# A decode kernel's output row: two column groups instead of four, the residual added on TensorE, the copy split over two engines, and two one-row stores

## The chip, the cores and the metric

The kernel runs on one core of a Trainium2 chip. A core has a matrix engine (PE, with its weight loads shown apart as PEld), a vector engine (DVE), a scalar engine (ACT), a general engine (POOL), a sequencer that mostly issues transfers (SP), and 16 DMA engines that move data between the chip's memory (HBM) and the on-chip memory (SBUF). Matmul results land in a separate accumulation memory, PSUM, which DVE and ACT read. Engines run their own instruction streams and wait for each other on semaphores.

The metric is the device time of one execution in microseconds. Before the change it is 128.65 us (median of three runs, 128.65 to 128.98). The profile is of another single execution, which took 128.68 us.

## What is computed

One token is decoded through two branches that share a normalised input, and both are added to the residual:

```python
xn = _layernorm(x)                       # x is (1, 1, 576)
# branch A: attention over the last W = 4096 cached positions, 32 query heads, 16 key/value heads
q = (xn @ wq).reshape(B, Sq, 32, 128)
p = _softmax(einsum(q, k[:, :, Sk - W:]) * 128 ** -0.5)
A = (einsum(p, v[:, :, Sk - W:])).reshape(B, Sq, 4096) @ wo
# branch B: a gated MLP
z = _gelu(xn @ w_in)                     # 4608 wide
z1, z2 = z[..., :2304], _layernorm(z[..., 2304:])
B = (z1 * (w_sp * z2 + b_sp)) @ w_out
out = x + A + B                          # (1, 1, 576), bfloat16
```

Nearly all of the work is reading: 16 heads of keys and of values (1 MB each), wq, w_in, w_out and wo come to 51 MB for one row of output.

## The kernel before

**Loads.** All large loads are issued by SP, in program order, into a ring of seven equal SBUF slots (`RING`, line 60): wq in two pieces, the first two pairs of K heads, w_in in three pieces, then pairs of K and V heads in turn (lines 83 to 86, issued at L85), w_out in one piece and wo in four pieces of 16, 10, 4 and 2 tiles (`load_n`, lines 88 to 91 and 105, issued at L90). A tile of wo is 128 rows of 576 columns; each partition of a piece of n tiles reads n x 1152 contiguous bytes. A load that reuses a slot waits until the engine that read the slot's old contents is done: DVE for a pair of K heads, PE for a pair of V heads. A slot is handed out in the order in which slots come free in the program. SP's queue is in order, so a load that waits holds back those behind it. The small loads go out from ACT's queue: x as 64 rows of 9 (`x64`), x as four rows of 144 (`x4`, lines 111 to 114, after a memset by DVE), and two scalars (`spb`).

**Main loop** (line 380, over 16 K heads). `t_head` (L247) transposes a K head with DVE, `s_head` (L255) makes scores on the PE, `sm_a` and `sm_b` do the softmax of a group of four heads with DVE and ACT, `pv` (L305) multiplies with V, and `yb` brings the group's result into `Y`. In between lies branch B: `z_mms` at head 3, `z_rest` at head 5, `z_norm` at head 6. `z_norm` sums over partitions with a matmul into a PSUM tile of its own, `psz`, taken from the pool `ps_m`, and ends in `hv`, the 2304 gated values. At head 5 the output accumulator `out_t`, 144 columns wide, is taken from the pool `ps_a` and zeroed (L393).

**The output.** The output row of 576 columns is kept as four groups of `CW` = 144 columns. `out_mms` (L403) multiplies one tile of w_out or wo, with one column of `hv` or `Y` as weights, in four matmuls, one for each group; group n writes partition 32n of `out_t`, and its `tile_position` puts it on a separate group of 32 columns of the PE array. After the loop come the last group's softmax, `yb(2)`, `pv(3)`, two thirds of w_out, `yb(3)`, the last third of w_out and the 32 tiles of wo, piece by piece as they land. The end is one DVE instruction (L425), which adds `x4` to `out_t` over 97 partitions and writes bfloat16, and one store from SP (L426) of the four rows at partitions 0, 32, 64 and 96.

**Order.** The kernel's order is written by hand (`manual_schedule`): each engine runs its instructions as the Python code issues them. The waits between engines are put in by the tile framework. It also gives the transfers eight semaphores in turn; a transfer waits until the earlier one on its semaphore has landed.

Of the kernel before, what the change touches and what calls it, by code (L numbers as in the profile page):

```python
# [8 lines left out]
FP32 = mybir.dt.float32  # L9
BF16 = mybir.dt.bfloat16  # L10
ALU = mybir.AluOpType
# [3 lines left out]
D = 576  # L15
# [11 lines left out]
NG = HKV // GK  # L27
NR = 98
NF = FH // 128
CW = D // 4  # L30
EPS = 1e-5
SCALE = DH ** -0.5
GELU_C = 0.7978845608028654
# [6 lines left out]
def kernel(  # L40
# [14 lines left out]
    nc = tc.nc  # L55
    P = nc.NUM_PARTITIONS

    const = ctx.enter_context(tc.tile_pool(name="const", bufs=1))
# [5 lines left out]
    ps_m = ctx.enter_context(tc.tile_pool(name="ps_m", bufs=1, space=bass.MemoryType.PSUM))  # L64
    ps_a = ctx.enter_context(tc.tile_pool(name="ps_a", bufs=1, space=bass.MemoryType.PSUM))
# [3 lines left out]
    x_flat = A_x.flatten_outer_dims()  # L69
# [18 lines left out]
    def load_n(src, per, lo, n, name):  # L88
        v = ring_tile(f"{name}{lo}", n, D)
        nc.sync.dma_start(v, src.rearrange("(p t) n -> p t n", t=per)[:, lo:lo + n, :])  # L90
        return [(lo + t, v[:, t, :]) for t in range(n)]
# [10 lines left out]
        V.update(load_kv(A_v_cache, m, "v"))  # L102
    wout_sb = load_n(B_w_out, NF, 0, NF, "wout")
    wo_sb = []
    for n in (16, 10, 4, 2):
        wo_sb += load_n(A_wo, 32, len(wo_sb), n, "wo")


    x64 = const.tile([64, NS], BF16, name="x64")
    nc.scalar.dma_start(x64[:], x_flat.rearrange("o (m j) -> (o m) j", j=NS))  # L110
    x4 = const.tile([P, CW], BF16, name="x4")
    nc.vector.memset(x4[:], 0.0)
    nc.scalar.dma_start(x4[:].rearrange("(a b) n -> a b n", b=32)[:, 0, :],
                        x_flat.rearrange("o (a n) -> (o a) n", a=4))
    spb = const.tile([1, 2], BF16, name="spb")
    nc.scalar.dma_start(spb[:, 0:1], B_w_sp.flatten_outer_dims()[0:1, 0:1])
    nc.scalar.dma_start(spb[:, 1:2], B_b_sp.flatten_outer_dims()[0:1, 0:1])
# [10 lines left out]
    ones_b = const.tile([1, P], BF16, name="ones_b")  # L128
# [28 lines left out]
    for n in range(2):  # L157
        t = ps_s.tile([P, 2, 512], FP32, name=f"S{n}")
# [22 lines left out]
        out=junk[:], in0=x_col[:], in1=x_col[:], scale=1.0, scalar=0.0,  # L181
# [23 lines left out]
    for s, wv in wq_sb:  # L205
        for g in range(4):
            nc.tensor.matmul(  # L207
                qps[32 * g:32 * g + 2, :], lhsT=XT[:, s, :], rhs=wv[:, 512 * g:512 * (g + 1)],
                start=(s == 0), stop=(s == NS - 1), tile_position=(0, 32 * g),
# [12 lines left out]
    for k in range(4):  # L222
        for be in range(4):
            nc.tensor.matmul(
                qps2[:, k, be, :].rearrange("p (r g) -> p r g", r=2),
                lhsT=q_rep[0:NR, 2 * k + be // 2, be % 2].rearrange("p a d -> p (a d)"),
                rhs=idq, start=True, stop=True)
# [10 lines left out]
    Y = const.tile([P, 32], BF16, name="Y")  # L238
# [3 lines left out]
    def t_head(j):  # L242
        kT = ktpool.tile([P, NT, 2, 32, 2], BF16, name=f"kT{j}", tag="kT")
        src = K[j].rearrange("p t d -> p (t d)").bitcast(FP32)
        dst = kT[:].rearrange("p t b k e -> p (t b k e)").bitcast(FP32)
        for hf in range(2):
            nc.vector.transpose(dst[:, 1024 * hf:1024 * (hf + 1)], src[:, 1024 * hf:1024 * (hf + 1)])  # L247
        KT[j] = kT

    def s_head(j):  # L250
        g, i = divmod(j, GK)
        kv = KT.pop(j)[:].rearrange("p t b k e -> p b e t k")
        for hf in range(2):
            for be in range(4):
                nc.tensor.matmul(  # L255
                    S[g % 2][32 * i:32 * i + 8, hf, :],
                    lhsT=Qb[:, j, be].rearrange("p a h -> p (a h)"),
                    rhs=kv[:, be // 2, be % 2, 16 * hf:16 * hf + 16, :],
                    start=(be == 0), stop=(be == 3), tile_position=(0, 32 * i),
                )  # L260
# [13 lines left out]
    def sm_a(g):  # L274
        s = S[g % 2]
        nc.vector.tensor_reduce(out=mx[:, 0:1], in_=s[:], op=ALU.max, axis=mybir.AxisListType.XY)  # L276
        bk = spread(mx, mb, g, ALU.max, "m")
        nm = work.tile([P, 1], FP32, name=f"nm{g}", tag="nm")
        nc.vector.tensor_scalar_mul(nm[:], bk[:, 0:1], -SCALE)  # L279
        p = work.tile([P, 1024], BF16, name=f"p{g}", tag="p")  # L280
        nc.scalar.activation(p[:], s[:].rearrange("p a n -> p (a n)"), ACT.Exp, bias=nm[:, 0:1], scale=SCALE,  # L281
                             accum_out=lx[:, 0:1])
        st[g] = {"p": p}

    def sm_b(g):
        d = st[g]
        pt = work.tile([P, NT, 32], BF16, name=f"pt{g}", tag="pt")
        nc.vector.transpose(pt[:].rearrange("p t x -> p (t x)"), d["p"][:])  # L288
        lbk = spread(lx, lb, g, ALU.add, "l")
        rs = work.tile([P, 1], FP32, name=f"rs{g}", tag="rs")  # L290
        nc.vector.reciprocal(rs[:], lbk[:, 0:1])
        PT = work.tile([P, GK, NT, 2], BF16, name=f"PT{g}", tag="PT")
        pt4 = pt[:].rearrange("p t x -> p (t x)").bitcast(FP32).rearrange("p (t x) -> p t x", x=16)
        PT4 = PT[:].rearrange("p i t h -> p (i t h)").bitcast(FP32).rearrange("p (i t) -> p i t", i=GK)
        for i in range(GK):
            for a in range(4):
                nc.scalar.copy(PT4[32 * a:32 * a + 32, i, :], pt4[32 * i:32 * i + 32, :, a])  # L297
        d["PT"] = PT
        d["rs"] = rs
# [29 lines left out]
    def z_mms():  # L329
        zps = ps_a.tile([P, 2, NF], FP32, name="zps", tag="a")  # L330
        for s, wv in win_sb:
            wt = wv.rearrange("k (p t) -> k t p", t=NF)
            for t in range(NF):
                nc.tensor.matmul(zps[:, :, t], lhsT=wt[:, t, :], rhs=XT[:, s, :],  # L334
                                 start=(s == 0 and t == 0), stop=(s == NS - 1 and t == NF - 1),
                                 skip_group_check=True)
        return zps
# [21 lines left out]
        )  # L359
        return G, sz  # L360

    def z_norm(G, sz):
        psz = ps_m.tile([P, 512], FP32, name="psz", tag="m")
        nc.tensor.matmul(psz[:, 0:2], lhsT=ones_f[:], rhs=sz[:], start=True, stop=True)
        mz = const.tile([P, 4], FP32, name="mz")
        nc.vector.tensor_scalar_mul(mz[:, 0:2], psz[:, 0:2], 1.0 / FH)
        nc.vector.tensor_mul(mz[:, 2:3], mz[:, 0:1], mz[:, 0:1])
        nc.vector.tensor_sub(mz[:, 2:3], mz[:, 1:2], mz[:, 2:3])
        nc.vector.tensor_scalar_add(mz[:, 2:3], mz[:, 2:3], EPS)
        nc.gpsimd.tensor_tensor(out=mz[:, 3:4], in0=mz[:, 2:3], in1=mhalf[:], op=ALU.pow)  # L370
        zn = const.tile([P, NF], FP32, name="zn")
        nc.vector.tensor_scalar(out=zn[:], in0=G[:, 1], scalar1=mz[:, 0:1], scalar2=mz[:, 3:4],
                                op0=ALU.subtract, op1=ALU.mult)
        nc.vector.tensor_scalar(out=zn[:], in0=zn[:], scalar1=wb[:, 0:1], scalar2=wb[:, 1:2],
                                op0=ALU.mult, op1=ALU.add)
        hv = const.tile([P, NF], BF16, name="hv")
        nc.vector.tensor_mul(hv[:], G[:, 0], zn[:])
        return hv

    for j in range(HKV):  # L380
        t_head(j)
        g, o = divmod(j, GK)
        if g > 0 and o == 0:
            sm_a(g - 1)
        if g > 0 and o == 1:
            sm_b(g - 1)
        s_head(j)
        if j == GK - 1:
            zps = z_mms()
        if j == GK + 1:  # L390
            G, sz = z_rest(zps)
            out_t = ps_a.tile([P, CW], FP32, name="out_t", tag="a")
            nc.vector.memset(out_t[:], 0.0)  # L393
        if j == GK + 2:
            hv = z_norm(G, sz)
        if g > 1 and o == 0:
            yb(g - 2)
        if g > 0 and o == 3:
            pv(g - 1)

    def out_mms(lhs, col, wv, first, last):
        for n in range(4):
            nc.tensor.matmul(  # L403
                out_t[32 * n:32 * n + 1, :], lhsT=lhs[:, col:col + 1], rhs=wv[:, CW * n:CW * (n + 1)],
                start=first, stop=last, tile_position=(0, 32 * n),
            )

    def out_hv(c):
        for t, wv in wout_sb[6 * c:6 * c + 6]:
            out_mms(hv, t, wv, t == 0, False)  # L410

    g = NG - 1
    sm_a(g)
# [1 line left out]
    yb(g - 1)  # L415
    pv(g)
    out_hv(0)
    out_hv(1)
    yb(g)
    out_hv(2)  # L420
    for t, wv in wo_sb:
        out_mms(Y, t, wv, False, t == 31)

    res = const.tile([P, CW], BF16, name="res")
    nc.vector.tensor_tensor(out=res[0:97, :], in0=out_t[0:97, :], in1=x4[0:97, :], op=ALU.add)  # L425
    nc.sync.dma_start(out.flatten_outer_dims().rearrange("o (a n) -> (o a) n", a=4),  # L426
                      res[:].rearrange("(a b) n -> a b n", b=32)[:, 0, :])


# [1 line left out]
_INS = ['A_x', 'A_k_cache', 'A_v_cache', 'A_wq', 'A_wo', 'B_x', 'B_w_in', 'B_w_sp', 'B_b_sp', 'B_w_out']  # L431
# [26 lines left out]
```

## Time and profile before

| what | value |
|---|---|
| median of three runs | 128.65 us (128.65 to 128.98) |
| the profiled execution, its own time | 128.68 us |
| its span, first to last instruction | 126.9 us |
| PE busy, PEld busy | 70.5 us (56%), 32.5 us (26%) |
| DVE busy | 74.1 us (58%) |
| ACT busy | 22.9 us (18%) |
| bytes read from HBM | 50.96 MB, 402 GB/s over the span |
| wo pieces: issued at | 91.51, 98.10, 101.22, 101.6 us |
| last store: issued at | 124.37 us |

The profile gives one row for a group of like instructions: source line, engine, operation, output and inputs, shapes and count. In a timeline the first two columns are the start in the span and the duration, and the bracket says how long the engine had been idle and what ended it. In the chain of waits each row is a piece of the path that ended last, with its start and its length; "issue" is time in which nothing is seen to be waited for. A digit in the row of 40 slices is a busy share in tenths. A view by stretches gives busy time by engine, the clock granted to the PE as a share of full speed, and the share of the DMA engines' time in use.

### The profile page before, as it was taken

To read this page: it belongs to the slowest core of one execution; us is meant where nothing else is said; L and a number is where in the kernel's file an instruction comes from. 1 tells how busy PE (TensorE), PEld (TensorE's weight loads), DVE (VectorE), ACT (ScalarE), POOL (GpSimd) and SP (SyncE) were. 2 spreads that over 40 slices of the span, in tenths; PEclk is the share of its full clock that TensorE was granted. 3 is DMA by queue.
4 is the path that set the end of the run, shared out by engine and by line. 5 is a ranking of instruction groups with operands and counts; after the bars stand their busy time and mean duration, and the time that the engine had idled before them with its cause. 6 is when DMAs were issued, how large, how long until landed. Compare 5 with 4: busy or idle time off the path is not lost.

```text
span 126.9 us, 1775 instructions
## 1 busy us (share of the span) xinstructions
PE 70.5 (56%) x708; PEld 32.5 (26%) x708; DVE 74.1 (58%) x157; ACT 22.9 (18%) x76; POOL 3.6 (3%) x19
## 2 busy tenths in 40 slices
PE   0002831399999796008359456991579901862460
PEld 0002301132699621002113111231113301222350
DVE  6704145999000499455399799997999557050000
ACT  0300011000000003930000308303074039200000
POOL 3401000000000000000100000000000000000000
PEclk9999996579985559955868976999555996589755
DMA  4999999999999999999999999999999999999940
GB/s 136 433 409 429 408 429 434 444 436 418 427 413 431 418 426 429 421 431 434 421 436 423 424 436 423 429 424 421 429 431 423 431 452 442 427 418 413 415 171 0
DMA packets 5899, 51.06 MB, mean 402 GB/s; under 512 B 516, under 2 KB 516, under 8 KB 772
## 3 DMA queue, kind: packets, MB, share of 16 engines
q1 hardware_dynamic: 5800, 50.96, 95.2%
q8 instruction: 5, 0.08, 0.2%
q10 hardware_dynamic: 92, 0.00, 0.0%
q14 instruction: 2, 0.02, 0.0%
HBM read 50.96 MB, written 0.00 MB: 402 GB/s over the span
## 4 chain that ended last, share of the span: by engine, by line
issue 41%; DVE 27%; DMA 25%; PE 3%; POOLq 0%; POOL 0%
DMA wo<-in_A_wo_dram 18%; DVE kT L247 16%; DMA x<-in_A_x_dram 7%; PE out_t L403 2%; DVE mx L276 2%; DVE pt L288 2%; DVE on L319 2%; DVE om L315 1%; PE yps L322 1%; PE ps_x L184 0%; POOLq L453 0%; POOL mv L190 0%; DVE mt L265 0%; DVE lb L271 0%; DVE mb L271 0%
## 5 line engine op out<-in xcount | busy, mean ns | idle before, releaser
L255 PE MATMUL S<-kT,Qb 128*8 128x512 bf16 x128 | 40.5, 484 | 21.8 <-DVE kT L247 21.0
L247 DVE STREAM_TRANSPOSE kT<-k 128x1024 f32<-128x1024 f32 x32 | 37.0, 1211 | 10.8 <-DMA k<-in_A_k_cache_dram 10.8
L255 PEld LDWEIGHTS <-Qb 128*8 128x8 bf16 x128 | 11.7, 98 | 46.7 <-issue 38.5
L297 ACT COPY PT<-pt 32x32 f32<-32x32 f32 x64 | 15.4, 241 | 13.7 <-DVE pt L288 12.9
L281 ACT ACTIVATE p<-S,nm 128x1024 bf16<-128x1024 f32 x4 | 4.5, 1113 | 54.8 <-DVE nm L279 54.8
L305 PE MATMUL ops<-v,PT 128*8 128x512 bf16 x128 | 13.3, 453 | 0.4 <-ACT PT L297 0.4
L334 PEld LDWEIGHTS <-win 128*128 128x128 bf16 x162 | 10.1, 164 | 0.4 <-issue 0.4
L334 PE MATMUL zps<-XT,win 128*128 128x2 bf16 x162 | 10.2, 202 | 0.0
L322 PE MATMUL yps<-on,sel 128*32 128x32 f32 x32 | 2.1, 220 | 10.8 <-DVE on L319 10.8
L403 PE MATMUL out_t<-wo,Y 128*1 128x144 bf16 x128 | 3.7, 276 | 5.2 <-DMA wo<-in_A_wo_dram 5.2
L276 DVE TENSOR_REDUCE mx<-S 128x1 f32<-128x1024 f32 x4 | 4.8, 1204 | 1.6 <-PE S L255 1.6
L425 DVE TENSOR_TENSOR res<-out_t,x 97x144 bf16<-97x144 f32 x1 | 0.3, 308 | 9.1 <-PE out_t L403 9.1
L288 DVE STREAM_TRANSPOSE pt<-p 128x1024 bf16<-128x1024 bf16 x4 | 4.8, 1210 | 1.4 <-ACT p L281 1.4
L305 PEld LDWEIGHTS <-PT 128*8 128x8 bf16 x128 | 4.0, 91 | 5.8 <-issue 2.0
L174 PE MATMUL ps_x<-x,rmat 64*128 64x9 bf16 x1 | 0.2, 163 | 9.5 <-DMA x<-in_A_x_dram 9.5
L315 DVE SCALAR_TENSOR_TENSOR om<-ops,rs,dmask 128x512 f32<-128x512 f32 x4 | 3.0, 742 | 4.2 <-PE ops L305 4.2
L322 PEld LDWEIGHTS yps<-on,sel 128*32 128x32 f32 x32 | 1.7, 132 | 12.5 <-DVE on L319 10.4
L403 PEld LDWEIGHTS <-Y 128*1 128x1 bf16 x128 | 2.9, 97 | 6.0 <-issue 5.9
L207 PE MATMUL qps<-wq,XT 128*2 128x512 bf16 x36 | 3.8, 603 | 0.8 <-DVE XT L198 0.8
L319 DVE TENSOR_REDUCE on<-om 128x128 f32<-128x512 f32 x4 | 4.1, 1023 | 0.1
L218 DVE CAST q_rep<-qps 128x512 bf16<-128x512 f32 x2 | 1.4, 692 | 4.4 <-PE qps L207 3.7
L216 ACT CAST q_rep<-qps 128x512 bf16<-128x512 f32 x2 | 1.2, 585 | 14.2 <-DVE q_rep L218 14.2
(88 smaller groups left out, 35.0 us busy)
## 6 DMA issues: line engine op xcount, KB each, us to landing
k<-in_A_k_cache_dram SPq DMA_DIRECT2D x8, 2048.0 KB, 24.9
v<-in_A_v_cache_dram SPq DMA_DIRECT2D x8, 2048.0 KB, 21.7
win<-in_B_w_in_dram SPq DMA_DIRECT2D x3, 1728.0 KB, 20.6
wout<-in_B_w_out_dram SPq DMA_DIRECT2D x1, 2592.0 KB, 27.4
wq<-in_A_wq_dram SPq DMA_DIRECT2D x1, 2560.0 KB, 8.8
wo<-in_A_wo_dram SPq DMA_DIRECT2D x1, 2304.0 KB
wq<-in_A_wq_dram SPq DMA_DIRECT2D x1, 2048.0 KB, 13.0
wo<-in_A_wo_dram SPq DMA_DIRECT2D x1, 1440.0 KB
```

What stands on the lines that cost most here:

```text
L247: nc.vector.transpose(dst[:, 1024 * hf:1024 * (hf + 1)], src[:, 1024 * hf:1024 * (hf + 1)])
L255: nc.tensor.matmul(S[g % 2][32 * i:32 * i + 8, hf, :], lhsT=Qb[:, j, be].rearrange("p a h -> p (a h)"), rhs=kv[:, be // 2, be % 2, 16 * hf ...
L276: nc.vector.tensor_reduce(out=mx[:, 0:1], in_=s[:], op=ALU.max, axis=mybir.AxisListType.XY)
L281: nc.scalar.activation(p[:], s[:].rearrange("p a n -> p (a n)"), ACT.Exp, bias=nm[:, 0:1], scale=SCALE, accum_out=lx[:, 0:1])
L288: nc.vector.transpose(pt[:].rearrange("p t x -> p (t x)"), d["p"][:])
L297: nc.scalar.copy(PT4[32 * a:32 * a + 32, i, :], pt4[32 * i:32 * i + 32, :, a])
L305: nc.tensor.matmul(ops[32 * i:32 * i + 8, :], lhsT=d["PT"][:, i, 4 * tb:4 * tb + 4, :].rearrange("p t h -> p (t h)"), rhs=V[GK * g + i][:, ...
L315: nc.vector.scalar_tensor_tensor(out=om[:].rearrange("p c d -> p (c d)"), in0=ops[:], scalar=d["rs"][:, 0:1], in1=dmask[:].rearrange("p c ...
L319: nc.vector.reduce_sum(on[:], om[:].rearrange("p c d -> p d c"), axis=AXX)
L322: nc.tensor.matmul(yps[32 * g:32 * g + 32, :], lhsT=sel[:, dq, :], rhs=on[:, 32 * dq:32 * dq + 32], start=(dq == 0), stop=(dq == 3), tile_ ...
L334: nc.tensor.matmul(zps[:, :, t], lhsT=wt[:, t, :], rhs=XT[:, s, :], start=(s == 0 and t == 0), stop=(s == NS - 1 and t == NF - 1), skip_gr ...
L403: nc.tensor.matmul(out_t[32 * n:32 * n + 1, :], lhsT=lhs[:, col:col + 1], rhs=wv[:, CW * n:CW * (n + 1)], start=first, stop=last, tile_pos ...
```

## The change

The output row is kept as two groups of 288 columns instead of four of 144, so `out_mms` issues two matmuls for a tile. The accumulator tile takes a whole bank of 512 columns, `acc`; its first 288 are `out_t`, and two further columns replace `psz` in `z_norm`. The residual x is loaded as one row on one partition and put into the accumulator by two matmuls with a weight of one, right after `z_norm`; those open the accumulation, so all later matmuls only add. wo comes in six pieces of 9, 8, 6, 4, 3 and 2 tiles. At the end DVE copies the left half of each group's columns and ACT the right half, both into `res`, and two stores of one row each go out, one from SP and one from ACT.

```diff
-CW = D // 4
+CW = D // 2
-    for n in (16, 10, 4, 2):
+    for n in (9, 8, 6, 4, 3, 2):
         wo_sb += load_n(A_wo, 32, len(wo_sb), n, "wo")
-    x4 = const.tile([P, CW], BF16, name="x4")
-    nc.vector.memset(x4[:], 0.0)
-    nc.scalar.dma_start(x4[:].rearrange("(a b) n -> a b n", b=32)[:, 0, :],
-                        x_flat.rearrange("o (a n) -> (o a) n", a=4))
+    xrow = const.tile([1, D], BF16, name="xrow")
+    nc.scalar.dma_start(xrow[:], x_flat)
-    def z_norm(G, sz):
-        psz = ps_m.tile([P, 512], FP32, name="psz", tag="m")
+    def z_norm(G, sz, psz):
...
-            out_t = ps_a.tile([P, CW], FP32, name="out_t", tag="a")
-            nc.vector.memset(out_t[:], 0.0)
+            acc = ps_a.tile([P, 512], FP32, name="acc", tag="a")
+            out_t = acc[:, 0:CW]
+            nc.vector.memset(out_t, 0.0)
         if j == GK + 2:
-            hv = z_norm(G, sz)
+            hv = z_norm(G, sz, acc[:, 384:386])
+            for n in range(2):
+                nc.tensor.matmul(
+                    out_t[32 * n:32 * n + 1, :], lhsT=ones_b[:, 0:1], rhs=xrow[:, CW * n:CW * (n + 1)],
+                    start=True, stop=False, tile_position=(0, 32 * n),
+                )
...
-    def out_mms(lhs, col, wv, first, last):
-        for n in range(4):
+    def out_mms(lhs, col, wv, last):
+        for n in range(2):
             nc.tensor.matmul(
                 out_t[32 * n:32 * n + 1, :], lhsT=lhs[:, col:col + 1], rhs=wv[:, CW * n:CW * (n + 1)],
-                start=first, stop=last, tile_position=(0, 32 * n),
+                start=False, stop=last, tile_position=(0, 32 * n),
             )
...
     res = const.tile([P, CW], BF16, name="res")
-    nc.vector.tensor_tensor(out=res[0:97, :], in0=out_t[0:97, :], in1=x4[0:97, :], op=ALU.add)
-    nc.sync.dma_start(out.flatten_outer_dims().rearrange("o (a n) -> (o a) n", a=4),
-                      res[:].rearrange("(a b) n -> a b n", b=32)[:, 0, :])
+    half = CW // 2
+    nc.vector.tensor_copy(res[0:33, 0:half], out_t[0:33, 0:half])
+    nc.scalar.copy(res[0:33, half:CW], out_t[0:33, half:CW])
+    out_row = out.flatten_outer_dims()
+    nc.sync.dma_start(out_row[:, 0:CW], res[0:1, :])
+    nc.scalar.dma_start(out_row[:, CW:D], res[32:33, :])
```

More of the change, by code (lines that the diff above doesn't have):

```diff
@@ L409, in out_hv @@
         for t, wv in wout_sb[6 * c:6 * c + 6]:
-            out_mms(hv, t, wv, t == 0, False)
+            out_mms(hv, t, wv, False)
     g = NG - 1
@@ L421 @@
     for t, wv in wo_sb:
-        out_mms(Y, t, wv, False, t == 31)
+        out_mms(Y, t, wv, t == 31)
     res = const.tile([P, CW], BF16, name="res")
-    nc.vector.tensor_tensor(out=res[0:97, :], in0=out_t[0:97, :], in1=x4[0:97, :], op=ALU.add)
-    nc.sync.dma_start(out.flatten_outer_dims().rearrange("o (a n) -> (o a) n", a=4),
-                      res[:].rearrange("(a b) n -> a b n", b=32)[:, 0, :])
+    half = CW // 2
[4 more added lines that the diff above has]
+    nc.scalar.dma_start(out_row[:, CW:D], res[32:33, :])
 _INS = ['A_x', 'A_k_cache', 'A_v_cache', 'A_wq', 'A_wo', 'B_x', 'B_w_in', 'B_w_sp', 'B_b_sp', 'B_w_out']
```

## The prediction

> **What bounds the kernel now.** I read the page first for the share of each engine and of the DMA queues, then the chain of waits to see what ends last, then stretches of the tail for clock and DMA share, and the timeline of the start for rows that price the changed operations.
>
> ```profile
> DMA  4999999999999999999999999999999999999940
> q1 hardware_dynamic: 5800, 50.96, 95.2%
> ...
> 98.10 23.38 DMA wo<-in_A_wo_dram
> 121.48 0.04 issue
> 121.52 1.37 PE out_t L403 x30
> 122.89 0.65 PE out_t L403 x13
> 123.54 0.03 issue
> 123.57 0.44 PE out_t L403 x8
> 124.03 0.31 DVE res L425
> ```
>
> The first row: the DMA engines are full from the second slice to the last but two; queue q1, the loads from SP, takes 95.2% of the span. Only 5% is left to anything else, so no compute edit before the last load counts unless it starves that queue. The second part is the end of the chain: the pieces of wo land at 121.48, 122.85 and 123.53, and after each the PE runs that piece's matmuls. The last piece (2 tiles, 8 matmuls) takes 0.44 us, the DVE add 0.31, and from 124.37 the store runs to the end of the span at 126.90. These 3.4 us after 123.53, and the landing itself, are all the change can touch.
>
> ```profile
> 118.00:119.00 1.00, 0.90 (x60) 0.90 (x63) 0.00 (x0) 0.00 (x0) 0.00 (x0) 1.00 1.05 449
> 119.00:120.00 1.00, 0.39 (x20) 0.18 (x7) 0.00 (x0) 0.00 (x0) 0.00 (x0) 0.50 0.86 359
> ...
> 122.00:123.00 1.00, 1.00 (x40) 0.79 (x32) 0.00 (x0) 0.00 (x0) 0.00 (x0) 0.50 0.23 90
> 123.00:124.00 1.00, 0.95 (x24) 0.43 (x16) 0.00 (x0) 0.00 (x0) 0.00 (x0) 0.50 0.01 5
> ```
>
> Columns: stretch, its length, busy time and count of PE, PEld, DVE, ACT, POOL, then granted clock, DMA share, GB/s. The clock falls from 1.00 to 0.50 at 119 and stays there. In 122 to 123 the DMA share is 0.23: most engines are done and a few stragglers still carry the last pieces.
>
> ```profile
> 17.02 0.69 DVE L218 CAST q_rep<-qps 128x512 bf16<-128x512 f32 x1 [3.72 <-PE qps L207]
> 17.75 0.58 ACT L216 CAST q_rep<-qps 128x512 bf16<-128x512 f32 x1 [13.44 <-DVE q_rep L218]
> 18.36 0.69 DVE L218 CAST q_rep<-qps 128x512 bf16<-128x512 f32 x1 [0.65 <-ACT q_rep L216]
> ...
> 1.34 1.06 ACTq L113 DMA_DIRECT2D x<-in_A_x_dram  x1
> 2.43 0.27 ACTq L116 DMA_DIRECT2D spb<-in_B_w_sp_dram  x1
> ...
> 124.37 0.65 SPq L426 DMA_DIRECT2D out_dram<-res  x1
> ```
>
> Two engines copying from one PSUM tile into one SBUF tile take turns, with 0.03 to 0.04 us between them. And a transfer of four rows holds its issuer 1.06 (load) or 0.65 us (store), while one of a single row takes 0.27.
>
> **The sum, against the profiled execution:** 128.68 us, of which 126.90 is the span and 1.78 lies around it; the runs shown have a median of 128.65, so nothing is corrected.
>
> *Landing of the last piece: +0.10.* Six pieces of wo instead of four mean two more packets for each of 128 partitions, 16 per DMA engine. In the trace's packet records 2304 B takes 93 ns and 4608 B 178, so 85 ns for the bytes and 8 for a packet: 16 x 8 = 0.13. Packets that follow each other overlap by 3 to 4 ns, which gives 0.08 as the low end, 0.15 as the high.
>
> *The two last pieces are late to issue: 0.* Their ring slots are those of the last two V tiles, free when the last pv ends (its last matmul starts at 111.70 and takes 0.62: 112.32). Behind them SP holds only the store. The first four pieces carry 27 of 32 tiles. The 10-tile piece landed 3.42 us after the one before, 0.342 a tile, so the stream needs the missing five tiles 1.7 us before the fast engines end at 121.4: about 119.7. The store shows 1.24 us from issue to first packet (124.37 to 125.60 in the packet records); the pieces could start by 114. About 5 us of queued wo hides the wait; without this cover each us late would be one us on the end.
>
> *Matmuls of the last piece: -0.02 at full clock, +0.26 at half.* The column groups run side by side: 40 matmuls of 144 columns (10 tiles) take 1.16 us of weight loads at clock 0.50, so 0.116 a tile, not four times that. Two groups of 288 columns double it: 0.232, still under the 0.342 at which tiles arrive, so the PE keeps up. At half clock the last piece takes 0.232 for its first tile and 0.328 + 0.116 for its second (the longest 144-column row plus its doubled columns): 0.68 against 0.44, and 0.02 more because the three-tile piece needs 0.70 and the next lands 0.68 later. At full clock the 144-column row is 0.223 and the 512-column rows at 82 us are 0.38 to 0.39, so 288 columns take about 0.29 and the piece 0.12 + 0.29 + 0.01 = 0.42. I take full: the halved number of groups doubles the columns streamed per arriving tile, 0.12 us in 0.342 instead of 0.06, and pieces of 9 to 2 tiles spread them; the stretch around 112 to 116 kept a clock of 0.98 with such a load (2.06 us of busy PE in four), while 1.29 us of PE in 116 to 119.4 did not.
> [...]
>
> *Evacuation: +0.36.* Removed: the DVE add, 0.31. Added: a DVE copy and an ACT copy of 144 columns each, the same width as before, since the rows are twice as long. In the built program ACT's copy waits for DVE's copy, not for the PE, and both stores wait for ACT: one after the other. DVE: 32 columns from PSUM took 0.187, 512 took 0.692, so 144 take 0.31. ACT: 32 columns took 0.241, 512 from PSUM 0.585, so 0.32. With two hand-overs of 0.04 and 0.03 the store issues 0.72 after the matmuls instead of 0.36. Ends: +0.28 (0.241 for ACT) to +0.45.
> [...]
>
> *Store issue: -0.38.* One store of four rows held SP 0.645. Two of one row go out from SP and ACT at the same time, each like the one-element load on ACT: 0.265. Ends: 0 (a store is no faster than the old one) to -0.39 (0.253, the other such load). The first packet may follow sooner too: up to -0.2.
>
> *Completion: +0.06.* Two semaphores are waited for at the end, each check 0.06 us apart in SP's records. Ends 0 and 0.1.
>
> *Hidden, at nothing:* the two residual matmuls and the DVE read before them sit where the PE then idles 3.49 us (until 64.99); uncovered they would cost 0.9. The memset of 288 columns is some 0.15 us longer on a DVE that is 58% busy, with K loads issued 24.9 us before they land. The x row and the scalars behind it issue 0.8 us sooner on ACT; XT, not they, opens the q matmuls at 13.17. 36 fewer w_out matmuls of twice the width end before the first wo piece (nine tiles, landing near 115.7).
>
> Sum: 0.10 + 0 - 0.02 + 0.36 - 0.38 + 0.06 = +0.12, so 128.80. The two large terms cancel.
>
> **Rivals.** *Slower: half clock at the end.* Place: the PE after the last landing. It decides if the window that holds 119 to 122 again counts as light. For it: the row at 119. Against: doubled columns. Price +0.28: 129.08; with a store issue that gains nothing, 129.46. Chance 0.29.
> *Faster: the stragglers vanish.* The landings of the last piece spread over 1.88 us by engine, with steps at 0.6, 1.13 to 1.33 and 1.81 to 1.88. The packet records show five 16 KB instruction packets (at 36.0, 43.1, 82.3, 111.4, 121.3), each about 0.9 us, after which one engine runs late for good. PE has 196 instructions less. If the last fetches then miss the slowest engines, the end moves up by 1.88 - 1.33 = 0.55: 128.25. Against: the first fetch alone made such a straggler, and nothing before it changes. Chance 0.11.
> *The halves do run side by side,* as the words say: 128.80 - 0.36 = 128.44. The program's wait excludes it nearly: 0.02.
> *The two late pieces starve the queue.* It decides if pv ends after about 118; it ended at 112.32. One us late would be 129.8. Chance 0.03.
> *The forecast, the tail's terms cancelling at full clock:* 128.80, chance 0.55; its own range 128.45 to 129.1 with the ends above.
>
> **How the numbers follow.** 0.3% of 128.65 is 0.39 us, about what a measurement of this kernel can tell from no change: "same" is 128.26 to 129.04. Predicted 128.80. The range reaches down to the faster rival's neighbourhood and up over the half-clock case: 128.30 to 129.25. Faster: the straggler case and a little of the low bounds, 0.13. Slower: most of the half-clock case, the starved queue and the top of the forecast, 0.31. Same: 0.56.
>
> **What would show it.** The last wo landing near 123.6; the last matmul 0.42 us later at clock 1.00, or 0.7 at 0.50; DVE's copy, then ACT's, back to back, 0.3 each; two stores of about 0.27 us on SP and ACT at one time. Wrong if ACT's copy overlaps DVE's, if the stores hold their queues for 0.6 us again, if the DMA share dips between 113 and 121, or if the spread of the last landings changes by more than 0.3 us.

## The result, and the profile after

The changed kernel takes 130.05 us (median of six runs, 129.86 to 130.34); the kernel before, run beside it, 128.65 us (six runs, 128.56 to 128.98). The ratio is 1.0107, with a 95% interval of 1.0093 to 1.012. The forecast of 128.80 us and its range, up to 129.25, lie below every run. The profiled execution, the slowest of the six, took 130.34 us with a span of 128.6; before it was 128.68 and 126.9. All ratios are taken over fast runs; one slow run of the kernel before, 160.81 us beside experiments 5 to 8, is left out of them.

The page of the changed kernel, first the row of 40 slices and the load queue:

```profile
DMA  5999999999999999999999999999999999999940
...
q1 hardware_dynamic: 6082, 50.96, 95.3%
...
HBM read 50.96 MB, written 0.00 MB: 396 GB/s over the span
```

The same bytes, the same share of the DMA engines' time (95.2% before), but 396 GB/s instead of 402. The engines are as full as they were and move less. To see that this isn't an effect of the ends, take one stretch in the middle, 20 to 110 us, in which only loads run that the change does not touch. Its columns are those of the prediction's stretches; the last two are DMA share and GB/s. First before, then after:

```profile
20.00:110.00 90.00, 57.79 (x441) 25.62 (x439) 64.08 (x123) 20.46 (x73) 0.55 (x1) 0.75 1.01 429
```

```profile
20.00:110.00 90.00, 57.61 (x437) 25.90 (x441) 64.27 (x123) 20.49 (x74) 0.55 (x1) 0.75 1.01 423
```

Busy times of PE, DVE and ACT, the granted clock and the DMA share are the same within 0.4 us in 90. Only the rate has fallen, by 1.4%. So the loss is not in the tail where the change works. It grows along the stream. Counted in the packet records, the first pair of heads is in at 18.64 us before and 18.79 after, the eighth pair at 65.48 and 66.19, the fifteenth at 99.92 and 101.08, the last piece of wo at 123.53 and 125.25. (The first 0.15 is of another kind: every packet of that pair takes 309 ns in both kernels.)

The end of the chain of waits of the changed kernel (start, length, what):

```profile
109.87 3.18 PE ops L303 x27
113.05 0.02 issue
113.07 0.33 SPq L90
...
113.46 0.03 issue
113.49 11.76 DMA wo<-in_A_wo_dram
125.25 0.04 issue
125.29 0.43 PE acc L406 x4
125.72 0.02 issue
125.74 0.31 DVE res L429
126.05 0.02 issue
126.07 0.27 ACT res L430
```

Read alone, this chain accuses the pieces of wo: the last ones are issued only at 113.07 to 113.49, when the last `pv` has set their slots free, and the end hangs on one of them. But 11.76 us from issue to landing is time in a full queue. The stretches around it show no gap:

```profile
113.00:114.00 1.00, 0.43 (x5) 0.00 (x0) 0.53 (x1) 0.00 (x0) 0.00 (x0) 0.86 1.06 435
114.00:115.00 1.00, 0.74 (x13) 0.52 (x14) 0.96 (x2) 0.00 (x0) 0.00 (x0) 1.00 0.93 392
...
121.00:122.00 1.00, 0.99 (x10) 0.40 (x5) 0.00 (x0) 0.00 (x0) 0.00 (x0) 0.50 0.98 395
...
125.00:126.00 1.00, 0.51 (x6) 0.09 (x3) 0.26 (x1) 0.00 (x0) 0.00 (x0) 1.00 0.00 0
```

The DMA share stays between 0.93 and 1.06 from 113 to 122 (experiment 7 tests the late pieces by themselves). The clock of the PE is 0.50 at 121, but 1.00 for the last piece. The tail in the timeline of the changed kernel:

```profile
125.74 0.30 DVE L429 CAST res<-acc 33x144 bf16<-33x144 f32 x1 [9.54 <-PE acc L406]
126.07 0.27 ACT L430 CAST res<-acc 33x144 bf16<-33x144 f32 x1 [16.25 <-DVE res L429]
126.37 0.32 SPq L432 DMA_DIRECT2D out_dram<-res  x1
126.37 0.23 ACTq L433 DMA_DIRECT2D out_dram<-res  x1
```

ACT is released by DVE, as forecast, and the two stores go out together. From the last landing to the end of the span the tail is 3.31 us (128.56 - 125.25), before 3.37 (126.90 - 123.53). So the change's own work gained 0.06 us in this pair of traces, and the landing lost 1.72. Part of the 1.72 belongs to this one execution: the engine that is done first with the last piece lands it 1.48 us later (121.64 and 123.12), the last one 1.72, and the medians of the times are 1.40 apart.

**The cause, from the packet records.** The trace holds size and duration of every DMA packet. Mean of those of the load queue, by size, and the sum per DMA engine over all of 1 KB or more (counted from the records; a packet is what one record of a transfer covers, here a contiguous run of bytes for one partition):

```
packet        8192 B    20736 B    13824 B    4608 B     sum per engine
before        309.6 ns  771.0      516.0      178.0      120.56 us
after         314.0     774.6      520.5      180.4      122.20
```

In the kernel before 4,086 of the 4,096 K and V packets take exactly 309 ns; after the change 1,322 do, and nearly all the others scatter up to 325. The sum grows by 1.64 us per engine, nearly the 1.72 of the landing. Not all packets are longer. The first three transfers, wq in two pieces and the first pair of K heads, are as before: the packets of wq keep their medians of 761 and 611 ns, and all 256 of the pair take 309. The first longer K packet starts at 18.54 us, in the second pair. And short packets lengthen less: 2304 bytes go from 93.0 to 93.9 ns.

What the change alters for an untouched K load is where it is written. The pool of constants lies ahead of the ring in SBUF, and the change makes two of its tiles larger: `x4`, 288 bytes a partition, gives way to `xrow`, 1152, and `res` doubles from 288 to 576. That is 864 + 288 = 1152 bytes, or 4 x 256 + 128. In the built programs the ring starts at byte 44288 of a partition before (173 x 256) and at 45440 after (177 x 256 + 128). A slot is 20736 bytes, 81 x 256, so all seven slots share the offset: multiples of 256 before, 128 past one after.

### The profile page after: what moved, and what is told of

Its sections match the earlier page's. It is cut to its first block, busy times and chain, and to the rows that moved or that the text cites. A ratio compares the mean times of both kernels' runs of the same rounds, so it can differ in the third digit from the quotient of the medians.

```text
span 128.6 us, 1586 instructions
## 1 busy us (share of the span) xinstructions
PE 74.6 (58%) x610; PEld 33.4 (26%) x610; DVE 74.2 (58%) x156; ACT 23.2 (18%) x77; POOL 3.6 (3%) x19
## 4 chain that ended last, share of the span: by engine, by line
issue 41%; DMA 28%; DVE 15%; PE 8%; ACT 4%; POOLq 0%; POOL 0%; SPq 0%; ACTq 0%; DVEq 0%
DMA k<-in_A_k_cache_dram 12%; DMA wo<-in_A_wo_dram 9%; DMA x<-in_A_x_dram 7%; DVE kT L245 6%; PE S L253 4%; ACT PT L295 3%; PE ops L303 2%; DVE pt L286 2%; DVE mx L274 2%; ACT p L279 1%; DVE on L317 1%; DVE om L313 1%; PE yps L320 1%; PE ps_x L182 0%; POOLq L458 0%
## 5 line engine op out<-in xcount | busy, mean ns | idle before, releaser
L406 PE MATMUL acc<-wo,Y 128*1 128x288 bf16 x64 | 6.3, 348 | 2.8 <-DMA wo<-in_A_wo_dram 2.7
```

The lines of the kernel that those rows point to most:

```text
L406: nc.tensor.matmul(out_t[32 * n:32 * n + 1, :], lhsT=lhs[:, col:col + 1], rhs=wv[:, CW * n:CW * (n + 1)], start=False, stop=last, tile_pos ...
```

## The experiments

**1. The changed kernel with the ring moved back to a multiple of 256.** An unused constant of 128 bytes a partition, which nothing writes or reads, ahead of the ring; nothing else.

```diff
+    pad = const.tile([P, 64], BF16, name="pad")
     ident = const.tile([P, P], BF16, name="ident")
```

> The changed kernel with 128 unused bytes a partition ahead of the ring, so that its slots start on multiples of 256 bytes again, as before the change. Theory 1 (every load packet is longer because the ring moved to 128 bytes past a multiple of 256): 8192-byte packets back from 314.0 to about 309.6 ns on average, last wo landing near 123.6, 128.7 us (128.5 to 128.9). Theory 2 (the last two wo pieces, issued 11 us later, or the six pieces): unchanged, 129.9 to 130.2, packets still 314 ns. Theory 3 (PE matmuls of 288 columns and the new copies disturb the loads): unchanged too.

Measured: 128.57 us (128.46 to 128.82, 11 runs), ratio to the kernel before 0.9998 (0.9989 to 1.0007). The stretch of its trace:

```profile
20.00:110.00 90.00, 58.36 (x444) 25.82 (x444) 64.14 (x123) 20.45 (x73) 0.55 (x1) 0.75 1.01 428
```

The rate is back, the K and V packets are at 309.6 ns, the last piece lands at 123.32. A tile that does no work takes 1.5 us off: the whole loss. What is left of the change can't be told from no change at all. This kernel is called the realigned kernel from here on. The sum per engine, 120.68, is 0.12 above that of the kernel before: those are the packets of two more pieces.

**2 to 4. The kernel before with the ring moved by 128, 256 and 64 bytes.** The same line, with 64, 128 and 32 columns of two bytes.

```diff
+    pad = const.tile([P, 64], BF16, name="pad")
     ident = const.tile([P, P], BF16, name="ident")
```

> The kernel before, with nothing but 128 unused bytes a partition ahead of the ring: slots 128 bytes past a multiple of 256. Theory 1: packets of 8192 bytes near 314 ns, loads 1.3 to 1.4% slower over some 118 us, so 129.9 to 130.3 us. Theories 2 and 3: 128.65, no change.

> Control: the kernel before with 256 unused bytes, all later tiles moved, slots still on multiples of 256. Theory 1: 128.65 as before, packets 309.6 ns. If moving the tiles as such (DVE, PE or ACT operands) were the cause: about 130.

> The kernel before with 64 unused bytes: slots 64 bytes past a multiple of 256. [...]

Measured: 128 bytes 130.02 us (129.92 to 130.18), ratio 1.0105 (1.0091 to 1.0119), packets 313.9 ns; 256 bytes 128.55 us, ratio 0.9993 (0.9984 to 1.0002), packets 309.5 ns; 64 bytes 130.05 us, ratio 1.0109 (1.0095 to 1.0123), packets 314.1 ns. With 128 bytes the stretch shows

```profile
20.00:110.00 90.00, 57.36 (x442) 25.77 (x443) 64.07 (x123) 20.47 (x73) 0.55 (x1) 0.75 1.02 424
```

The old kernel, with one unused tile and no other edit, becomes as slow as the changed one, and twice the tile makes it fast again. So it isn't the presence of a tile, nor its size: it is where the tiles behind it start modulo 256, and 64 costs what 128 does. The pad moves the ring, the pools `work` and `ktpool` and most constants together; experiments 9 and 10 take these apart. As after the change, all 256 packets of the first pair of K heads still take 309 ns at 64 and at 128 bytes.

**5. Two PSUM banks, so that the copies can overlap.** In the realigned kernel the left halves of both rows accumulate in `acc`, the right halves in a bank of their own, in four matmuls of 144 columns for a tile.

```diff
+            acc2 = ps_b.tile([P, 512], FP32, name="acc2")
+            outs = [acc[:, 0:HW2], acc2[:, 0:HW2]]
...
-    nc.vector.tensor_copy(res[0:33, 0:half], out_t[0:33, 0:half])
-    nc.scalar.copy(res[0:33, half:CW], out_t[0:33, half:CW])
+    nc.vector.tensor_copy(res[0:33, 0:half], outs[0][0:33, :])
+    nc.scalar.copy(res[0:33, half:CW], outs[1][0:33, :])
```

> The aligned changed kernel (128 unused bytes), with the left and the right halves of the two output rows in two PSUM banks (four matmuls of 144 columns a tile, still two column groups), so that ACT's copy waits for the PE and not for DVE. Theory 1: the loads are untouched, packets 309.6 ns, and the copies run side by side: 0.33 us from the last matmul to the stores instead of 0.65, so 128.57 - 0.3 = about 128.25 us, the first version under both kernels. Rival (the wait comes from the shared output tile, or the copies slow each other): 128.5 to 128.6.

Measured: 128.35 us (128.18 to 129.01, 12 runs), ratio 0.9982 (0.9967 to 0.9998). Its tail:

```profile
123.81 0.30 DVE L438 CAST res<-acc 33x144 bf16<-33x144 f32 x1 [9.16 <-PE acc L414]
123.87 0.27 ACT L439 CAST res<-acc 33x144 bf16<-33x144 f32 x1 [15.40 <-PE acc L414]
124.17 0.32 SPq L441 DMA_DIRECT2D out_dram<-res  x1
124.19 0.23 ACTq L442 DMA_DIRECT2D out_dram<-res  x1
```

ACT now waits for the PE, not for DVE, and starts 0.06 us after it. The stores issue 0.36 us after DVE starts; in experiment 1 it is 0.63:

```profile
123.81 0.30 DVE L430 CAST res<-acc 33x144 bf16<-33x144 f32 x1 [8.87 <-PE acc L407]
124.15 0.27 ACT L431 CAST res<-acc 33x144 bf16<-33x144 f32 x1 [15.42 <-DVE res L430]
124.44 0.32 SPq L433 DMA_DIRECT2D out_dram<-res  x1
```

The medians differ by 0.22 us (128.57 - 128.35), near the 0.27 between the two tails; 128.35 lies between the two expectations, nearer the first. The two kernels differ in the number of matmuls too, but the tails show where the time lies. Each half has now a tile of its own as well as a bank of its own; no run shows which of the two the program's wait goes by.

**6. One copy by DVE.** The realigned kernel, with all 288 columns copied by DVE and none by ACT.

```diff
-    nc.vector.tensor_copy(res[0:33, 0:half], out_t[0:33, 0:half])
-    nc.scalar.copy(res[0:33, half:CW], out_t[0:33, half:CW])
+    nc.vector.tensor_copy(res[0:33, :], out_t[0:33, :])
```

> The aligned changed kernel, with one DVE copy of all 288 columns in place of the two halves. From 1.04 ns a column and 0.16 fixed, 0.46 us and one hand-over, 0.51 from last matmul to stores against 0.65: about 128.43. Rival (handing over costs nothing that matters, or the stores decide): 128.57.

Measured: 128.47 us, ratio 0.9986 (0.9974 to 0.9998).

```profile
123.97 0.45 DVE L430 CAST res<-acc 33x288 bf16<-33x288 f32 x1 [9.37 <-PE acc L407]
124.45 0.31 SPq L432 DMA_DIRECT2D out_dram<-res  x1
```

A line through the DVE add of 144 columns (0.308 us) and the copy of 512 (0.692) in the trace of before gives the expectation's 1.04 ns a column and 0.16 fixed. One copy of 288 columns takes 0.45 us, and the store issues 0.48 after DVE starts. Sharing the copy, as the change does it, needs 0.63: here the second engine cost 0.15 us more than it saved. That reading rests on the two tails: the medians are 0.10 us apart, and the intervals of the two ratios overlap.

**7. Four pieces of wo instead of six,** in the realigned kernel.

```diff
-    for n in (9, 8, 6, 4, 3, 2):
+    for n in (16, 10, 4, 2):
```

> The aligned changed kernel with wo in four pieces of 16, 10, 4 and 2 tiles as before. If the late issue of the two last pieces costs nothing and 256 more packets cost 0.1 us: 128.45 to 128.6, last landing within 0.2 us. If the six pieces had cost or gained more, it shows here: 128.2 or 128.9.

Measured: 128.48 us, ratio 0.9985 (0.9973 to 0.9997), within 0.09 us of six pieces. No piece waits for the last `pv` here, and the last landing is at 123.41, against 123.32 with six. So the late issue that the chain shows costs nothing. The size of the pieces matters little either way. The profiled execution, 128.77 us, lies above the median and shows what half clock cost there: the clock is 0.50 from 120 to 122 us, the PE falls behind and ends at 124.16, 0.75 us after the last landing, where in experiment 1, at clock 1.00, it ends 0.47 after it (123.79).

**8. The kernel before, moved by 32 bytes.** The line of experiment 2 with 16 columns.

```diff
+    pad = const.tile([P, 16], BF16, name="pad")
     ident = const.tile([P, P], BF16, name="ident")
```

> The kernel before with 32 unused bytes: slots 32 bytes past a multiple of 256. If any start off a multiple of 256 costs the same: 130.0, 8192-byte packets 314 ns. [...]

Measured: 130.42 us (two runs, 130.38 and 130.46), ratio 1.0131 (1.0102 to 1.016), packets 314.8 ns. It lies above the 130.0 expected for an equal cost. The penalty at 32 bytes is a little larger than at 64 or 128, 5.2 ns a packet against 4.5 and 4.3; why it is larger stays open.

**9 and 10. Is it the ring, and only its start?** Experiment 9 opens the ring's pool ahead of the constants in the changed kernel; experiment 10 puts the 128 unused bytes behind the ring in the kernel before.

```diff
+    ring = ctx.enter_context(tc.tile_pool(name="ring", bufs=RING))
     const = ctx.enter_context(tc.tile_pool(name="const", bufs=1))
     work = ctx.enter_context(tc.tile_pool(name="work", bufs=2))
-    ring = ctx.enter_context(tc.tile_pool(name="ring", bufs=RING))
```

> The changed kernel with the ring's pool opened ahead of the pool of constants, nothing else. In the built program the ring's slots move from 45440 to 16512 bytes (64 x 256 + 128), so they lie on wholly other addresses but again 128 past a multiple of 256, and the constants lie behind the ring. Theory (only the start of the destination modulo 256 counts): as slow as the changed kernel, 130.05 us (129.8 to 130.3), 8192-byte packets at 314 ns. Rival (the constants' new layout, or the ring's place in SBUF, costs the time): the sum of constants ahead of the ring is gone, so about 128.6.

```diff
     ring = ctx.enter_context(tc.tile_pool(name="ring", bufs=RING))
+    behind = ctx.enter_context(tc.tile_pool(name="behind", bufs=1))
...
+    pad = behind.tile([P, 64], BF16, name="pad")
     ident = const.tile([P, P], BF16, name="ident")
```

> The kernel before with the unused 128 bytes per partition in a pool of their own behind the ring, so the ring stays at 44288 bytes (173 x 256) and only the transposed K tiles behind it move by 128. Theory (the ring's start alone): no change, 128.65 us (128.4 to 128.9), packets at 309.6 ns. Rival (the 128 bytes cost time wherever they lie, through the engines that read the shifted tiles): 130.0, as the same pad ahead of the ring gave.

Measured: ring first, 130.15 us (129.97 to 130.18, 4 runs), ratio 1.0113 (1.01 to 1.0127), packets 314.0 ns; pad behind the ring, 128.58 us (10 runs), ratio 1.0003 (0.9992 to 1.0015), packets 309.6 ns. The stretch of experiment 9:

```profile
20.00:110.00 90.00, 57.29 (x441) 25.53 (x445) 64.26 (x123) 20.51 (x73) 0.55 (x1) 0.77 1.01 423
```

Every slot lies 28,928 bytes lower than in the changed kernel, and the time is the same, since 16512 is again 128 past a multiple of 256. The 128 bytes cost nothing where they leave the ring in place. Both rivals fall as they were put: it isn't the room that the constants take ahead of the ring, nor the shift of the transposed K tiles. In experiment 9 the constants and `work` keep their starts modulo 256, though, and in every run with longer packets `work` is as far off a multiple as the ring. The traces settle whether the engines' reading and writing of such tiles takes part. In experiment 2 no engine runs an instruction from 115.28 to 119.24 us, and the 101 packets of wo inside that stretch still last 3.7 ns longer on average than those of the kernel before (432 ns for 11520 bytes, 686 for 18432). In the kernel before, in a like stretch from 115.04 to 118.10, none of 82 is longer. So what counts is the start of the ring.

**11. The parts that gain, together:** ring on a multiple of 256, two banks, four pieces.

```diff
-    for n in (9, 8, 6, 4, 3, 2):
+    for n in (16, 10, 4, 2):
```

(against experiment 5)

> The changed kernel with the ring back on multiples of 256, the two halves of each row in two PSUM banks, and wo in pieces of 16, 10, 4 and 2 tiles as before the change. If the two gains add, 128.35 (two banks, six pieces) less 0.09 (four pieces instead of six: 128.48 against 128.57) gives 128.26 us. Rival (four pieces gain nothing, the difference of 0.09 was chance): 128.35. Either way below the kernel before, 128.65 to 128.69. If the clock falls to half at the end, as in the profile of the four-piece run, up to 128.6.

Measured: 128.21 us (128.08 to 128.28, 5 runs), the kernel before beside it 128.57; ratio 0.9963 (0.9951 to 0.9976). It is faster than both kernels, by 0.36 us than the one before. The sum of the two gains was put at 128.26; that four pieces add something of their own is not shown, since the kernel before was itself 0.12 us faster beside this run than beside experiment 5 (128.57 and 128.69). Its tail has the overlap of experiment 5:

```profile
123.83 0.30 DVE L438 CAST res<-acc 33x144 bf16<-33x144 f32 x1 [9.40 <-PE acc L414]
123.89 0.27 ACT L439 CAST res<-acc 33x144 bf16<-33x144 f32 x1 [15.32 <-PE acc L414]
124.19 0.32 SPq L441 DMA_DIRECT2D out_dram<-res  x1
```

## Why the prediction was wrong

**The step that failed is the landing of the last piece: +0.10 forecast, +1.72 measured.** Its count of packets was right. The realigned kernel with six pieces has 0.12 us more packet time per engine than the kernel before, against the 0.13 reckoned before overlap. What failed is that all packets were taken, without a reason given, to last as long as before. They carry the same bytes by the same queue, so a price by size alone seemed safe. But 4.4 ns on each of 4,096 K and V packets is 256 x 4.4 = 1.13 us per engine, and the other 96 packets of an engine bring the rest of the 122.20 - 120.68 = 1.52 us between the changed and the realigned kernel (0.14 of it from a few long packets of the first piece of wq, whose median is the same in both).

**The omission sits in "hidden, at nothing".** The x row was priced there as a transfer on ACT's queue, and the doubled `res` not at all. Neither was priced for the room that it takes in SBUF, ahead of the ring. No rival held this, so no chance was given to it; the range was worked out from the tail and had no way to reach 130.

**The tail was right in size, term by term.** From the last landing to the end, forecast and measured change:

| term | forecast | measured | from |
|---|---|---|---|
| matmuls of the last piece | -0.02 (0.42) | -0.01 (0.43) | 125.29 to 125.72, clock 1.00; before 0.44 |
| evacuation, until the store issues | +0.36 (0.72) | +0.29 (0.65) | 125.72 to 126.37; before 0.36 |
| store issue and completion | -0.38 + 0.06 | -0.34 | 126.37 to 128.56 is 2.19; before 2.53 |
| sum | +0.02 | -0.06 | 3.31 against 3.37 |

The full clock of the first row was in part luck. The reason given was that the new pieces keep the PE busy enough. The stretch from 116.6 to 120.0 us held 1.31 us of busy PE, hardly more than the 1.29 in 3.4 us that the prediction names for before, and the clock fell to 0.50 at 120 all the same. It was back at 1.00 at 123.5, ahead of the last piece at 125.29, which was itself late. In experiment 1, with the same pieces, it stayed at 1.00 from 119 to 124. That busier pieces keep the clock was the author's estimate from two stretches; how much work keeps it, no run shows.

The evacuation was 0.07 too high: ACT's copy of 144 columns took 0.27, not 0.32, between its low bound of 0.241 and the value taken. The forecast took the wait between the copies from the built program. Experiment 5 shows it by itself: with a tile and a bank for each half it is gone, and the stores issue 0.36 us after DVE starts, against 0.63 in experiment 1. No run shows what an overlap within one tile or one bank would do.

One reading under "hidden" was wrong and cost nothing: the x row was to issue 0.8 us sooner, since one row held its issuer 0.27. Those 0.27 were of one-element loads; the load of the whole row held ACT 0.68 us, 0.38 less than the four rows before.

**The late issue of the last two pieces: right.** They were issued at 113.07, forecast by 114; the DMA share does not dip, and experiment 7 without late pieces lands them no earlier.

**Rivals.** Half clock at the end did not come for the last piece, as said above. Its price of +0.28 fits experiment 7's profiled execution (0.75 - 0.47 = 0.28), though the clock there was back at 1.00 by 123 us and the PE was only late. The starved queue did not come either. The spread of the last landings by engine was 2.13 us instead of 1.88, within the 0.3 allowed; it was 1.62 in experiment 1, so it varies between runs. The stragglers did not vanish: an instruction fetch at 124.5 us still falls into the tail. Overlapping halves were rightly given almost no chance, and experiment 5 shows that they are to be had, for about 0.22 us.

## What to carry to other kernels

This kernel is bound by its loads, and the address of its buffers belonged to the cost of an edit: 128 unused bytes ahead of the ring took 1.05% more time (experiment 2), 256 none (ratio 0.9993, experiment 3). So in a kernel of this kind add up the bytes per partition of what a change adds, removes or resizes ahead of the streamed buffers, see whether their starts stay multiples of 256, and if not, measure a pad that brings them back; here it took 1.5 us off (experiment 1). A small constant moves the starts, and so does the order in which pools are opened (experiment 9: from 45440 to 16512). The sign in this profile was a DMA share as full as before (1.01) with fewer GB/s (423 instead of 429), in a stretch that the change does not touch; the chain of waits did not show it, since it names the load that came last, here a piece of wo.

## What the runs showed of the hardware

- With the ring 32, 64 or 128 bytes past a multiple of 256, load packets from the second pair of heads on last a few ns longer, in no clear order of size from 8 KB up. On average 8192 bytes go from 309.6 to between 313.9 and 314.8 ns; in the changed kernel, 128 past, 10368 bytes from 392.9 (experiment 1) to 394.4, 13824 bytes from 516.0 to 520.5, 20736 bytes from 771.0 to 774.6, and 4608 bytes from 178.0 to 180.4. For this kernel it is 1.05 to 1.3% of the time.
- The offset alone is not enough. The first three transfers have it too and show nothing: all 256 packets of the first pair of K heads take 309 ns at 64 and at 128 bytes past, and 253 of them at 32. Their slots, used again later, do cost more: each of the other 15 pairs of heads takes at least 2.7 ns a packet more on average.
- Packets that don't go to the ring are longer too. A packet of 8192 bytes on the instruction queue, at 46.3 to 47.3 us, took 309 ns in all eight runs with the ring on a multiple of 256 (before, 1, 3, 5, 6, 7, 10, 11) and 325 to 328 in the other five. So the cost isn't a property of the single packet; that packets on the way at the same time hold each other up would fit, and is not shown.
- The start of the source in HBM showed no such cost with the ring on a multiple of 256. Pieces of 4 tiles take 178.0 ns a packet both where they begin at tile 26 (before, a multiple of 256 bytes from the start of wo) and at tile 23 (experiment 1, 128 past one).
- What takes the few ns, and what sets it in at the second pair, is not shown. A small extra for each packet that hardly grows with size (4.4 ns at 8192 bytes, 3.6 at 20736) would fit the sizes from 8 KB up, but not the first three transfers, which pay nothing.
- The one-row stores of the changed kernel held SP 0.32 us and ACT 0.23, where the four-row store held SP 0.65. The one-row load of x held ACT 0.68, the four-row load 1.06.
